# One double load removed, two loads moved: rows of q, k and v in an attention and feed-forward kernel

## The chip, the cores and the metric

The kernel runs on one core of a Trainium2 chip. A core has a matrix engine (TensorE, PE), a vector engine (VectorE, DVE), a scalar engine (ScalarE, ACT), a general engine (GpSimd, POOL) and an engine that mostly issues transfers (SyncE, SP). Each runs its own list of instructions in order; they meet through semaphores. Sixteen DMA engines move data between the chip's memory (HBM) and the on-chip memory (SBUF); transfers are issued from the lists of SyncE, ScalarE and GpSimd. The metric is the device time of one execution in microseconds, as the median of several runs.

## The reference

Attention with a squared ReLU in place of softmax, over 8 batches of 12 heads, 448 positions and 64 elements a head; then a feed-forward layer with a leaky ReLU whose slope is different for each hidden unit.

```python
# q, k, v: (8, 12, 448, 64)
scores = scale * np.matmul(q, k.transpose(0, 1, 3, 2))
attn = np.maximum(scores, 0.0) ** 2 / S
attn_out = np.matmul(attn, v)
x = attn_out.transpose(0, 2, 1, 3).reshape(B * S, H * D)      # (3584, 768)
h = x @ w_in                                                 # (3584, 2048)
g = np.maximum(h, 0.0) + alpha * np.minimum(h, 0.0)
out = g @ w_out                                              # (3584, 768)
```

## The kernel before

The heads are worked on four at a time. Such a group is called a quad: with NG = 3 quads to a batch and 8 batches there are NQ = 24, numbered 0 to 23. Each quad passes through these steps.

Its rows are loaded by GpSimd, with a cast from float32 to bfloat16. q and k have three buffers each, v has seven:

```python
raw_pool = ctx.enter_context(tc.tile_pool(name="raw", bufs=3))
v_pool = ctx.enter_context(tc.tile_pool(name="v", bufs=7))
perm_pool = ctx.enter_context(tc.tile_pool(name="perm", bufs=2))
T_pool = ctx.enter_context(tc.tile_pool(name="T", bufs=4))
...
def load_qk(n):
    b, g = divmod(n, NG)
    for name, src in (("q", q), ("k", k)):
        t = raw_pool.tile([128, 2, NJ, D], BF16, tag=name, name=f"{name}raw")
        flat = src[b].rearrange("(m two) (pp j) d -> (two pp) m (j d)", two=2, j=NJ)
        nc.gpsimd.dma_start(out=t.rearrange("p m j d -> p m (j d)"), in_=flat[:, 2 * g:2 * g + 2])   # L91
        raw[(n, name)] = t

def load_v(n):                  # the same for v, into vraw[n]                                        # L98
    ...
```

Scores need q and k with the 64 elements of a head on the partitions, so both are transposed. Quads 0 to 5 are transposed by TensorE (`turn_pe`, L144, with copies out of PSUM at L147). Quads 6 to 23 are reordered by VectorE into a tile `perm` and transposed by a DMA that SyncE issues:

```python
def turn_dma(n):
    p = perm_pool.tile([128, 2, NJ, 2, D], BF16, tag="perm", name="perm")
    for i, name in enumerate("qk"):
        nc.vector.tensor_copy(p[:, i], raw.pop((n, name)).rearrange("p s j d -> p j s d"))            # L155
    t = T_pool.tile([128, 2, NJ, 128], BF16, tag="T", name="T")
    nc.sync.dma_start_transpose(out=t.rearrange("p a j c -> p (a j) c"),
                                in_=p.rearrange("p a j s d -> p (a j s d)"))                          # L157
    T[n] = t
```

Then come seven chunks of scores (`score_mm`, L169), a ReLU (L178 on ScalarE, L180 on VectorE), a square (L185), the product with v (`attnv`, L195), and once all three quads of a batch are there, the first layer (`f1`, matmuls at L229, outputs at L237 and L238) and the second (`f2`, matmuls at L252, a copy at L254, a store at L260).

The schedule is written out by hand, and TensorE's order is the order of the calls. The part that matters here is the end of the first phase, where batch 0's second layer and batch 1's attention meet, and the first-layer block of batch 1 behind it:

```python
def prepare(n):
    if n < NQ:
        turn_dma(n)
    if n + 2 < NQ:
        load_qk(n + 2)
        load_v(n + 2)
...
sc(ch(4, 5, 7))
turn_pe(5)
sq()
load_qk(8)                      # L347: quad 8
load_v(8)
f2(0, 1, 0)
...                             # scores of quad 5, attnv(4), more of f2
early = []
for ff in range(4):
    ps = take_bank()[:, :S]
    f1_mm(ps, 1, ff, range(4))
    early.append(ps)
    if ff == 1:
        attnv(5)
for ff in range(KF):            # KF = 16
    if ff < 4:
        f1_mm(early[ff], 1, ff, range(4, KM))
        f1_out(early[ff], 1, ff)
    else:
        f1(1, ff)
    if ff in (1, 5, 9):
        prepare(6 + ff // 4)    # turns quad 6, 7, 8; loads quad 8 (again), 9, 10
f2(0, 3, 0)
run(some(3))                    # scores of quad 6 and on, three chunks at a time
f2(0, 3, 1)
f2(0, 0, 1)
run(some(3))
f2(0, 1, 1)
run(some(3))
f2(0, 2, 1)
f2(0, 4, 0)
prepare(9)                      # L398: turns quad 9, loads quad 11
burst(6)                        # three chunks, attnv(6), three chunks
...
prepare(10)                     # turns quad 10, loads quad 12
burst(8)
...                             # batches 2 to 7 in the same manner
```

Quad 8 is loaded at L347, and once more by `prepare(6)`. The second tile replaces the first under `raw[(8, "q")]`, `raw[(8, "k")]` and `vraw[8]`, so the first is not read by anything.

Of the kernel before, what the change touches and what calls it, by code (L numbers as in the profile page):

```python
# [20 lines left out]
def kernel(  # L21
# [17 lines left out]
    NQ = B * NG  # L39
# [46 lines left out]
# [8 lines that stand above are left out]
    def load_v(n):  # L94
        b, g = divmod(n, NG)
        t = v_pool.tile([128, 2, NJ, D], BF16, tag="v", name="vraw")
        flat = v[b].rearrange("(m two) (pp j) d -> (two pp) m (j d)", two=2, j=NJ)
        nc.gpsimd.dma_start(out=t.rearrange("p m j d -> p m (j d)"), in_=flat[:, 2 * g:2 * g + 2])  # L98
        vraw[n] = t
# [52 lines left out]
# [8 lines that stand above are left out]
# [67 lines left out]
    def f1_mm(ps, b, ff, ks):  # L227
        for km in ks:
            nc.tensor.matmul(ps, w_in_sb[:, km // 2, km % 2, bass.ts(ff, 128)],  # L229
                             xT[b][:, km // 2, km % 2, :],  # L230
                             start=(km == 0), stop=(km == KM - 1))

    def f1_out(ps, b, ff):
        if b % 2 == 0 and ff == 0:
            gT[b // 2] = g_pool.tile([128, KF, 2 * S], BF16, tag="g", name="gT")
        neg = neg_pool.tile([128, S], F32, tag="neg", name="neg")
        nc.scalar.activation(neg, ps, ACTF.Relu, scale=-1.0)  # L237
        nc.vector.scalar_tensor_tensor(gT[b // 2][:, ff, (b % 2) * S:(b % 2) * S + S],  # L238
                                       neg, beta_sb[:, ff:ff + 1], ps, ALU.mult, ALU.add)
        sq(1)  # L240

    def f1(b, ff):
        ps = take_bank()[:, :S]
        f1_mm(ps, b, ff, range(KM))
        f1_out(ps, b, ff)

    def f2(sb, c, hf, parts=((0, HALF),)):
        o = o_pool.tile([128, HALF], F32, tag="o", name="osb")
        for lo, hi in parts:
            ps = take_bank()[:, :hi - lo]  # L250
            for ff in range(KF):
                nc.tensor.matmul(ps, gT[sb][:, ff, bass.ts(c, 128)], w_out_sb[:, hf, ff, lo:hi],  # L252
                                 start=(ff == 0), stop=(ff == KF - 1))
            nc.scalar.copy(o[:, lo:hi], ps)  # L254
            for u in range(2):
                blk = 2 * c + u
                b, j = 2 * sb + blk // NJ, blk % NJ
                rows = out[b * S:(b + 1) * S].rearrange("(pp j) d -> j pp d", j=NJ)
                eng = nc.scalar if u and hi - lo < HALF else nc.sync
                eng.dma_start(out=rows[j][:, hf * HALF + lo:hf * HALF + hi], in_=o[64 * u:64 * u + 64, lo:hi])  # L260
# [53 lines left out]
    def f1s(b, lo, hi):  # L314
        for ff in range(lo, hi):
            f1(b, ff)

    def prepare(n):
        if n < NQ:
            turn_dma(n)  # L320
        if n + 2 < NQ:
            load_qk(n + 2)
            load_v(n + 2)

    f1s(0, 2, 3)
    turn_pe(3)
# [54 lines left out]
    for ff in range(KF):  # L381
# [3 lines that stand above are left out]
        else:  # L385
            f1(1, ff)
        if ff in (1, 5, 9):
            prepare(6 + ff // 4)
    f2(0, 3, 0)
    run(some(3))  # L390
    f2(0, 3, 1)
# [4 lines left out]
    f2(0, 2, 1)  # L396
    f2(0, 4, 0)
    prepare(9)  # L398
    burst(6)
    f2(0, 4, 1)  # L400
    f2(0, 5, 0)
    burst(7)
    f2(0, 5, 1)
    f2(0, 6, 0)
    prepare(10)
    burst(8)
    f2(0, 6, 1)
# [56 lines left out]
```

## Time and profile before

| what | value |
|---|---|
| time, median of 3 runs | 392.98 us (392.55 to 398.75) |
| span of the profiled execution | 389.5 us |
| TensorE busy | 378.2 us, 97% |
| VectorE busy | 263.9 us, 68% |
| ScalarE busy | 207.5 us, 53% |
| GpSimd busy | 65.5 us, 17% |
| moved by DMA | 43.75 MB, 112 GB/s on average |
| GpSimd's DMA queue | 23.04 MB, 40.4% of the 16 engines' span |
| first DMA queue of SyncE and ScalarE | 19.65 MB, 25.7% |
| loads of q, k, v by GpSimd | 24, 24 and 25, of 224 KB each as written |
| median from issue to landing of those loads | 4.8, 6.7 and 7.4 us |
| transposing transfers | 18, 7.6 us median to landing (3.4 to 14.6) |

The profile is of one execution, and its times count from the first instruction. A line such as L91 is a line of the kernel. In the tables of waits and in timelines, an arrow points to what an engine waited for: the last event that released it. Busy time of TensorE (PE) is that of its matmuls; they are pipelined, so their mean duration (353 ns at L229) is longer than their spacing. A transfer has an issue, which takes time on the issuing engine, and a landing.

### The profile page before, as it was taken

To read this page: it belongs to the slowest core of one execution; us is meant where nothing else is said; L and a number is where in the kernel's file an instruction comes from. 1 tells how busy PE (TensorE), PEld (TensorE's weight loads), DVE (VectorE), ACT (ScalarE), POOL (GpSimd) and SP (SyncE) were. 2 spreads that over 40 slices of the span, in tenths; PEclk is the share of its full clock that TensorE was granted. 3 is DMA by queue.
4 is the path that set the end of the run, shared out by engine and by line. 5 is a ranking of instruction groups with operands and counts; after the bars stand their busy time and mean duration, and the time that the engine had idled before them with its cause. 6 is when DMAs were issued, how large, how long until landed. Compare 5 with 4: busy or idle time off the path is not lost.

```text
span 389.5 us, 7956 instructions
## 1 busy us (share of the span) xinstructions
PE 378.2 (97%) x3228; PEld 216.0 (55%) x3228; DVE 263.9 (68%) x418; ACT 207.5 (53%) x332; POOL 65.5 (17%) x97
## 2 busy tenths in 40 slices
PE   7779999999999999999999999999999999999996
PEld 5435454555665556645655456654666546655564
DVE  3977966865777777868756687878756786735300
ACT  4966566545546546555455554655644565524311
POOL 7557212520202040202202022102000000000000
PEclk9999999999999999999999999999999999999999
DMA  9999999996859089574939259490832311120023
GB/s 181 191 202 204 206 211 206 167 195 139 134 86 144 29 129 169 82 98 73 159 89 146 55 53 176 95 153 8 164 82 51 80 24 46 42 61 2 12 72 82
DMA packets 71909, 43.75 MB, mean 112 GB/s; under 512 B 38208, under 2 KB 71872, under 8 KB 71872
## 3 DMA queue, kind: packets, MB, share of 16 engines
q0 software_dynamic: 27312, 23.04, 40.4%
q1 hardware_dynamic: 44128, 19.65, 25.7%
q8 instruction: 25, 0.41, 0.4%
q10 hardware_dynamic: 432, 0.56, 0.4%
q14 instruction: 12, 0.10, 0.1%
HBM read 47.00 MB, written 11.01 MB: 149 GB/s over the span
## 4 chain that ended last, share of the span: by engine, by line
PE 88%; ACT 5%; DVE 3%; issue 2%; DMA 1%; ACTq 0%
PE psum L252 38%; PE psum L229 36%; PE psum L169 7%; PE psum L195 6%; ACT rl L178 4%; DVE at L185 2%; DMA qfirst<-in_q_dram 1%; DVE T L147 1%; PE psum L144 1%; ACT xT L205 1%; DVE rl L180 1%; DVE gT L238 0%; ACT osb L254 0%; DVE qraw L127 0%; ACTq L260 0%
## 5 line engine op out<-in xcount | busy, mean ns | idle before, releaser
L252 PE MATMUL psum<-w_out_sb,gT 128*128 128x384 bf16 (+2 forms) x912 | 150.7, 323 | 0.2
L229 PE MATMUL psum<-xT,w_in_sb 128*128 128x448 bf16 x768 | 148.7, 353 | 1.1 <-ACT xT L205 0.6
L252 PEld LDWEIGHTS <-gT 128*128 128x128 bf16 x912 | 87.6, 98 | 61.5 <-issue 6.7
L229 PEld LDWEIGHTS <-w_in_sb 128*128 128x128 bf16 x768 | 74.2, 98 | 71.8 <-issue 4.4
L238 DVE SCALAR_TENSOR_TENSOR gT<-neg,beta_sb,psum 128x448 bf16<-128x448 f32 x128 | 84.5, 678 | 41.3 <-ACT neg L237 40.9
L237 ACT ACTIVATE neg<-psum 128x448 f32<-128x448 f32 x128 | 69.3, 546 | 70.3 <-PE psum L229 64.7
L178 ACT ACTIVATE rl<-psum 128x896 bf16<-128x896 f32 x120 | 102.9, 928 | 1.2 <-PE psum L169 1.2
L185 DVE TENSOR_TENSOR at<-rl 128x896 bf16<-128x896 bf16 x168 | 94.1, 618 | 3.5 <-ACT rl L178 3.4
L254 ACT COPY osb<-psum 128x384 f32<-128x384 f32 (+2 forms) x57 | 27.0, 474 | 97.5 <-PE psum L252 94.0
L180 DVE TENSOR_SCALAR rl<-psum 128x896 bf16<-128x896 f32 x48 | 52.1, 1086 | 37.1 <-PE psum L169 37.1
L91 POOL DMA_DIRECT2D qraw<-in_q_dram x24 | 17.2, 718 | 190.2 <-DVE perm L155 170.1
L169 PE MATMUL psum<-T 64*64 64x448 bf16 x672 | 44.7, 355 | 3.8 <-DVE T L147 1.4
L195 PE MATMUL psum<-at,vraw 64*64 64x448 bf16 x672 | 37.9, 351 | 0.7 <-ACT rl L178 0.2
L169 PEld LDWEIGHTS <-T 64*64 64x64 bf16 x672 | 20.9, 105 | 21.6 <-issue 14.6
L195 PEld LDWEIGHTS <-vraw 64*64 64x64 bf16 x672 | 24.8, 106 | 10.9 <-issue 3.7
L206 DVE TENSOR_SCALAR xT<-psum 128x448 bf16<-128x448 f32 x22 | 13.7, 625 | 14.3 <-PE psum L195 7.2
L91 POOL DMA_DIRECT2D kraw<-in_k_dram x24 | 17.3, 721 | 6.9 <-PE psum L169 3.3
L98 POOL DMA_DIRECT2D vraw<-in_v_dram x25 | 18.0, 722 | 1.2 <-DMA w_in_sb<-in_moe_w_in_dram 0.4
L205 ACT ACTIVATE xT<-psum 128x448 bf16<-128x448 f32 x22 | 12.0, 545 | 5.4 <-PE psum L195 5.4
L155 DVE COPY perm<-qraw 128x896 bf16<-128x896 bf16 x18 | 11.0, 612 | 0.4 <-DMA T<-perm 0.4
L108 POOL DMA_DIRECT2D w_in_sb<-in_moe_w_in_dram x16 | 10.0, 628 | 7.4 <-DMA vraw<-in_v_dram 2.5
L155 DVE COPY perm<-kraw 128x896 bf16<-128x896 bf16 x18 | 11.0, 609 | 0.0
(19 smaller groups left out, 35.5 us busy)
## 6 DMA issues: line engine op xcount, KB each, us to landing
out_dram<-osb SPq DMA_DIRECT2D x110, 96.0 KB, 2.3
vraw<-in_v_dram POOLq DMA_DIRECT2D x25, 224.0 KB, 7.4
qraw<-in_q_dram POOLq DMA_DIRECT2D x24, 224.0 KB, 4.8
kraw<-in_k_dram POOLq DMA_DIRECT2D x24, 224.0 KB, 6.7
w_in_sb<-in_moe_w_in_dram POOLq DMA_DIRECT2D x16, 192.0 KB, 8.7
w_out_sb<-in_moe_w_out_dram POOLq DMA_DIRECT2D x2, 1536.0 KB, 18.6
qfirst<-in_q_dram SPq DMA_DIRECT2D x1, 448.0 KB, 4.4
kfirst<-in_k_dram ACTq DMA_DIRECT2D x1, 448.0 KB, 4.7
```

Of the source, the lines that this page charges most:

```text
L91: nc.gpsimd.dma_start(out=t.rearrange("p m j d -> p m (j d)"), in_=flat[:, 2 * g:2 * g + 2])
L155: nc.vector.tensor_copy(p[:, i], raw.pop((n, name)).rearrange("p s j d -> p j s d"))
L169: nc.tensor.matmul(ps[64 * c:64 * c + 64, r, :S], t[64 * r:64 * r + 64, 1, j, 64 * c:64 * c + 64], t[64 * r:64 * r + 64, 0, :, 64 * c:64 * ...
L178: nc.scalar.activation(rl, ps[:, :, :S], ACTF.Relu)
L180: nc.vector.tensor_scalar(rl, ps[:, :, :S], 0.0, None, ALU.max)
L185: nc.vector.tensor_tensor(a, rl, rl, ALU.mult)
L195: nc.tensor.matmul(ps[64 * s:64 * s + 64, r, :S], vv[64 * r:64 * r + 64, s, j, :], a[64 * r:64 * r + 64, s], start=(j == 0), stop=(j == NJ ...
L229: nc.tensor.matmul(ps, w_in_sb[:, km // 2, km % 2, bass.ts(ff, 128)], xT[b][:, km // 2, km % 2, :], start=(km == 0), stop=(km == KM - 1))
L237: nc.scalar.activation(neg, ps, ACTF.Relu, scale=-1.0)
L238: nc.vector.scalar_tensor_tensor(gT[b // 2][:, ff, (b % 2) * S:(b % 2) * S + S], neg, beta_sb[:, ff:ff + 1], ps, ALU.mult, ALU.add)
L252: nc.tensor.matmul(ps, gT[sb][:, ff, bass.ts(c, 128)], w_out_sb[:, hf, ff, lo:hi], start=(ff == 0), stop=(ff == KF - 1))
L254: nc.scalar.copy(o[:, lo:hi], ps)
```

## The change

The rows of quad 8 are loaded once instead of twice, and in the first-layer block of batch 1 the calls that load quads 9 and 10 stand after the three calls that transpose quads 6, 7 and 8, at ff = 13, where before each transposing call was followed by a load. The aim is to spare a transfer that nothing reads, and to let the three transposing transfers go without loads beside them. `prepare` keeps its meaning for quads 9 and later.

```diff
+    def load(n):
+        if n < NQ:
+            load_qk(n)
+            load_v(n)
+
     def prepare(n):
         if n < NQ:
             turn_dma(n)
-        if n + 2 < NQ:
-            load_qk(n + 2)
-            load_v(n + 2)
+        load(n + 2)
...
         else:
             f1(1, ff)
         if ff in (1, 5, 9):
-            prepare(6 + ff // 4)
+            turn_dma(6 + ff // 4)
+        if ff == 13:
+            load(9)
+            load(10)
     f2(0, 3, 0)
```

## The prediction

> **What bounds the kernel now.** I read the page from the top first: the busy shares, the strips of forty slices (9.7 us each), the chain that ended last.
>
> ```profile
> PE 378.2 (97%) x3228; PEld 216.0 (55%) x3228; DVE 263.9 (68%) x418; ACT 207.5 (53%) x332; POOL 65.5 (17%) x97
> ...
> PE   7779999999999999999999999999999999999996
> ...
> DMA  9999999996859089574939259490832311120023
> ...
> PE 88%; ACT 5%; DVE 3%; issue 2%; DMA 1%; ACTq 0%
> PE psum L252 38%; PE psum L229 36%; PE psum L169 7%; PE psum L195 6%; ACT rl L178 4%; DVE at L185 2%; DMA qfirst<-in_q_dram 1%; DVE T L147 1%; PE psum L144 1%; ACT xT L205 1%; DVE rl L180 1%; DVE gT L238 0%; ACT osb L254 0%; DVE qraw L127 0%; ACTq L260 0%
> ```
>
> TensorE is busy for 378.2 of 389.5 us, and 88% of the chain is TensorE; the only DMA in it is the first load of q. The DMA engines are also near full for the first nine slices, to about 88 us, so "the transfers are full" and "TensorE is full" are both on the page, and the stage that is changed has to decide between them. That stage is the first-layer block of batch 1 (L381 to L394) and what follows until quads 9 and 10 are used. The chain of waits in order of time shows it:
>
> ```profile
> 66.38 16.75 PE psum L229 x88
> 83.14 2.60 PE psum L252 x16
> 85.74 0.69 PE psum L169 x12
> 86.43 5.31 PE psum L252 x32
> ```
>
> 88 matmuls of the first layer without a break, then f2(0, 3, 0), then the first three score chunks of quad 6, then more f2. No step between them is a wait. The busy time by stretches says the same of the whole affected region (columns: stretch, its length, busy time and instructions of PE, PEld, DVE, ACT, POOL, granted clock, DMA share, GB/s):
>
> ```profile
> 66.00:83.20 17.20, 17.20 (x94) 8.90 (x94) 13.08 (x22) 8.45 (x17) 8.59 (x12) 1.00 1.12 177
> 83.20:122.60 39.40, 39.40 (x369) 23.58 (x368) 27.15 (x43) 21.28 (x32) 4.28 (x6) 1.00 0.76 131
> ```
>
> PE is busy for 17.20 of 17.20 and 39.40 of 39.40 us, at full clock. A wait that could be removed isn't there.
>
> Then I asked who issues and who waits. GpSimd's timeline gives each load's issue:
>
> ```profile
> 54.63 0.72 POOL L91 DMA_DIRECT2D qraw<-in_q_dram  x1 [5.05 <-PE psum L144]
> ...
> 66.72 0.72 POOL L91 DMA_DIRECT2D qraw<-in_q_dram  x1 [6.63 <-DMA qraw<-in_q_dram]
> 68.24 0.72 POOL L91 DMA_DIRECT2D kraw<-in_k_dram  x1 [0.80 <-DMA kraw<-in_k_dram]
> 68.95 0.72 POOL L98 DMA_DIRECT2D vraw<-in_v_dram  x1
> 71.10 0.72 POOL L91 DMA_DIRECT2D qraw<-in_q_dram  x1 [1.43 <-DVE perm L155]
> ...
> 74.52 0.72 POOL L91 DMA_DIRECT2D qraw<-in_q_dram  x1 [1.28 <-DVE perm L155]
> ...
> 78.95 0.72 POOL L91 DMA_DIRECT2D qraw<-in_q_dram  x1 [1.36 <-DVE perm L155]
> ```
>
> I matched these to the program's order: 54.63 is quad 8 (L347), 66.72 is quad 8 again, out of prepare(6). The first copy's tile is dropped unread, so the second takes the same buffer and has to wait 6.63 us for the first to land. 71.10 is quad 9, 74.52 quad 10, and 78.95 already quad 11, though prepare(9) stands far below in the text (L398). So GpSimd isn't paced by the place of a call among the matmuls. It runs through its own list and stops only where a buffer isn't free: with three buffers per name, quad 9 waits for the copy of quad 6 to perm (VectorE, 70.19 us), 10 for that of quad 7 (73.60), 11 for that of quad 8 (78.03).
>
> The last view is VectorE's timeline, with the only wait for a transposing transfer in the whole run:
>
> ```profile
> 70.19 0.61 DVE L155 COPY perm<-qraw 128x896 bf16<-128x896 bf16 x1
> ...
> 78.03 0.62 DVE L155 COPY perm<-qraw 128x896 bf16<-128x896 bf16 x1 [0.41 <-DMA T<-perm]
> ```
>
> **What the Trainium skill says.** "DMA: Bandwidth & Descriptors", section "Anatomy of one DMA — SWDGE (gpsimd) path", says that the DMA engines don't wait on semaphores: a wait happens on the issuing sequencer, before dispatch. The trace agrees: the GpSimd loads start right after the perm copy that frees their buffer (71.10 after a copy that runs from 70.19 to 70.80). The same page, "Queues, rings and completion order", says that each DMA engine goes round-robin over the queues that have work, packet by packet, so a load and a transposing transfer in flight together share the engines. The trace agrees as far as it goes: the three transposing transfers of quads 6 to 8, issued at 71.4, 74.8 and 80.3 us, took 6.5, 14.6 and 10.7 us to land, while the shortest of all 18 took 3.4 us. "SBUF — State Buffer", section "SBUF: two separate sides", lists TensorE's SBUF ports as its own, with contention only between VectorE and GpSimd or among DMA; a matmul should then not slow down under DMA traffic. Here the 88 matmuls under full DMA took 16.75 us, 190.3 ns each; 96 matmuls of the last batch (18.16 us, with the DMA digits at 1) took 189.2 ns each. That is 0.6%, or 0.1 us over the 88.
>
> **The change, part by part.** I compared the order of instructions, and the counts that each waits for, in the two built programs.
>
> *Removed:* one issue each of q, k and v, 3 x 0.72 us = 2.15 us of GpSimd, from 66.72 on, and the 6.63 us that it waited ahead of them. GpSimd then waits for the perm copy of quad 6 instead. The DMA work: the page's queue of GpSimd carries 23.04 MB in 40.4% of 389.5 us, 157.4 us, so 6.83 us per MB on all 16 engines; three times 224 KB is 0.69 MB, or 4.7 us of all engines, all between 66.7 and about 88 us. On the path: nothing, since TensorE has no gap there.
>
> *Moved:* the loads of quads 9 and 10, in the text. In the built programs, the q and k loads of quad 9 wait for VectorE's instructions 87 and 88 before and after; those of quad 10 for 93 and 94 in both; those of quad 11 for 99 and 100 in both. The order on PE, VectorE, ScalarE and SyncE is the same instruction for instruction; what differs in their waits is only which of eight numbered DMA semaphores a load signals. So quad 9 is still issued at about 71 and quad 10 at about 74.5 us, ahead of the landing of the transposing transfers at 77.9, 89.4 and 91.0 us (issue plus landing time), and not behind them. This half of the change is void: the place in the text doesn't hold a queue back, only a wait does.
>
> *Follows from it:* less traffic beside the three transposing transfers. They may land up to 4.7 us earlier in all. T of quad 6 landed at 77.9 and is first used at 85.7 us; quad 7 landed at 89.4 and is used at 95.1; quad 8 landed at 91.0 and is used at 103. Slacks of 7.8, 5.7 and 12 us: earlier is of no use. VectorE's wait of 0.41 us for perm's buffer may go; VectorE was idle for 4.1 of the 17.2 us in this stretch and TensorE didn't wait for it. SyncE's issues may be shorter (three transposes, 17.3 us of its queue), so the stores behind them start before 88.8 us; ScalarE doesn't wait for a store there.
>
> Sum: 0 on the path from the removed load, 0 from the move, 0 to 0.1 us from matmuls with less traffic beside them. 392.98 - 0.1 is 392.9; I say 392.8, with the rest for a small effect on the tail of VectorE that I can't work out.
>
> **The rivals.** *First: the doubled load keeps the chain back through the DMA engines.* For it: DMA digits of 9 up to 88 us, and a landing of 14.6 us. If quad 7's T were late, removing 4.7 us of traffic would give up to 4.7 us, 1.2%: about 388.3. Against it: PE busy 39.40 of 39.40 us and a slack of 5.7 us on the tightest of the three. It needs waits that this trace doesn't have.
>
> *Second: the later loads come too late.* If the loads did move behind quad 8's transposing transfer, they would be issued from about 81 us on, and quads 9 and 10 are copied to perm at about 98 and 116 us. With the median landing times of 4.8 to 7.4 us there would be some 10 us left even then. And if quad 11 were pushed back, it is needed later still. It makes the time longer only if a queue of loads builds up; I give that at most 1 us.
>
> *Third: a new collision.* Quad 8's q, k and v now come from the single load issued at 54.6 to 59.4 us. Its q had landed by 66.7 and its k by 68.2 us (the doubled loads waited for just that), some 10 us ahead of their use at 78.0. And v, with seven buffers, gets one more buffer of slack. Nothing for a slower time.
>
> **Range and chances.** Since no instruction of the four other engines changes its place, what decides is the spread between executions. Of the three runs before, two lie 0.43 us apart and the third 1.5% above; the profiled execution took 391.3 us. So plus and minus 1.2 us: 391.6 to 394.0. Faster by over 2% needs 7.9 us, more than twice TensorE's idle time after the first 66 us (11.3 us in all, 7.5 of it before 66 us): 0.01. Slower by over 2% needs a wait of 8 us that nothing here points to: 0.005. Within 2%: 0.985.
>
> **What would show it right or wrong.** Right: TensorE still busy for about 378.2 us and without a gap from 66 to 122 us; GpSimd busy for some 63.3 us, with 23 q loads, 23 k loads and 24 v loads; the issue at 66.72 gone, and the next still at about 71, 74.5 and 78.5 us, not at 81 or later; q, k and v queue at 22.35 MB; the three transposing transfers landing sooner than 6.5, 14.6 and 10.7 us, with TensorE indifferent to it. Wrong: loads of quad 9 issued after 80 us, a gap on TensorE before a score matmul (L169) put down to T, or a first-layer block that takes more or less than 16.75 us by over 0.3 us. The prediction would fail as a whole if traffic slows matmuls or their weight loads in a way that the busy time of PE hides.

## The result and the profile after

The changed kernel takes 391.43 us (median of 4 executions, 391.24 to 391.54). The kernel before, beside it, takes 393.24 us (4 executions, 392.55 to 398.75). The ratio is 0.9959, with a 95% interval of 0.994 to 0.9979: faster by 0.4%. Ratios here are taken over the executions within 1.5% of a kernel's fastest one; where I count executions, I count all.

The profile after hardly differs from the one before. First its page, the lines that answer to those shown of before:

```profile
span 389.7 us, 7952 instructions
...
PE 378.6 (97%) x3228; PEld 216.5 (56%) x3228; DVE 263.8 (68%) x418; ACT 207.5 (53%) x332; POOL 63.3 (16%) x94
...
DMA  9999999696859089574949269490932311120023
...
q0 software_dynamic: 26496, 22.35, 39.3%
```

The span is 389.7 us against 389.5. GpSimd lost 2.2 us of work, its queue 0.69 MB, and the eighth digit of the DMA strip (68 to 78 us) fell from 9 to 6. Next the GpSimd timeline of the changed kernel:

```profile
54.78 0.72 POOL L91 DMA_DIRECT2D qraw<-in_q_dram  x1 [5.02 <-PE psum L144]
...
71.25 0.72 POOL L91 DMA_DIRECT2D qraw<-in_q_dram  x1 [10.97 <-DVE perm L155]
...
74.67 0.72 POOL L91 DMA_DIRECT2D qraw<-in_q_dram  x1 [1.28 <-DVE perm L155]
...
79.22 0.72 POOL L91 DMA_DIRECT2D qraw<-in_q_dram  x1 [2.41 <-DVE perm L155]
```

The issue at 66.7 us is gone; quads 9, 10 and 11 are issued where they were. Last, the chain of waits of the changed kernel in the same stage:

```profile
66.53 16.75 PE psum L229 x88
83.29 2.60 PE psum L252 x16
85.89 0.69 PE psum L169 x12
86.58 5.31 PE psum L252 x32
```

Each piece is as long as before, to 0.01 us; all start 0.15 us later. VectorE's wait for perm's buffer is there too, 0.52 us instead of 0.41:

```profile
78.29 0.62 DVE L155 COPY perm<-qraw 128x896 bf16<-128x896 bf16 x1 [0.52 <-DMA T<-perm]
```

So the two profiled executions are equal, and the medians of plain executions are 1.8 us apart. A difference that one trace of each kernel can't show must lie in how executions of the same kernel differ. That is what the experiments are about.

### The profile page after: what moved, and what is told of

It is laid out like the page before. It is cut to its first block, busy times and chain, and to the rows that moved or that the text cites. A ratio compares the mean times of both kernels' runs of the same rounds, so it can differ in the third digit from the quotient of the medians.

```text
span 389.7 us, 7952 instructions
## 1 busy us (share of the span) xinstructions
PE 378.6 (97%) x3228; PEld 216.5 (56%) x3228; DVE 263.8 (68%) x418; ACT 207.5 (53%) x332; POOL 63.3 (16%) x94
## 3 DMA queue, kind: packets, MB, share of 16 engines
q0 software_dynamic: 26496, 22.35, 39.3%
## 4 chain that ended last, share of the span: by engine, by line
PE 87%; ACT 5%; DVE 3%; DMA 2%; issue 2%; ACTq 0%
PE psum L252 37%; PE psum L229 36%; PE psum L169 7%; PE psum L195 6%; ACT rl L178 4%; DVE at L185 2%; DMA qfirst<-in_q_dram 1%; DVE T L147 1%; PE psum L144 1%; ACT xT L205 1%; DVE rl L180 1%; DMA out_dram<-osb 1%; DVE gT L238 0%; ACT osb L254 0%; DVE qraw L127 0%
## 5 line engine op out<-in xcount | busy, mean ns | idle before, releaser
L229 PE MATMUL psum<-xT,w_in_sb 128*128 128x448 bf16 x768 | 148.6, 353 | 1.1 <-ACT xT L205 0.6
L229 PEld LDWEIGHTS <-w_in_sb 128*128 128x128 bf16 x768 | 74.2, 98 | 71.8 <-issue 4.4
L238 DVE SCALAR_TENSOR_TENSOR gT<-neg,beta_sb,psum 128x448 bf16<-128x448 f32 x128 | 84.3, 677 | 41.3 <-ACT neg L237 40.9
L169 PEld LDWEIGHTS <-T 64*64 64x64 bf16 x672 | 20.9, 105 | 21.6 <-issue 14.6
L91 POOL DMA_DIRECT2D kraw<-in_k_dram x23 | 16.6, 720 | 5.7 <-PE psum L169 3.4
```

Source lines behind the costliest of these rows:

```text
L169: nc.tensor.matmul(ps[64 * c:64 * c + 64, r, :S], t[64 * r:64 * r + 64, 1, j, 64 * c:64 * c + 64], t[64 * r:64 * r + 64, 0, :, 64 * c:64 * ...
```

## The experiments

Two theories at the start. *Traffic*: the useless load costs time in some executions of the kernel before that the profile of one good execution doesn't show. *Draw*: the kernel before is no slower, and three or four of its executions were unlucky.

**e1_same_again.** The kernel before, with no edit but a comment.

> The kernel before once more, as a kernel of its own: what two copies of one program differ by. If the measured 0.41% (1.8 us) belongs to the removed load, this copy gives a ratio of 1.000 within 0.15%, about 393.2 us. If the 0.41% lies in which executions of the kernel before were drawn, this copy comes out below the kernel before too, by 0.2% or more (392.5 us or less).

Measured: median 393.45 us over 22 executions, 391.21 to 401.27; ratio 1.001, 0.9976 to 1.0043. The kernel before on the same chip: 391.14 to 402.27 over 75, median 392.0. The figures fit the first expectation and not the second, but the interval is 0.7% wide, so this run can't tell a gain of 0.4% from none. What it shows is the width itself. The two copies share a floor of 391.2 us, 9 of 22 and 20 of 75 of their executions lie above 395 us, and over 75 executions the median of the kernel before is 392.0 us, not the 393.24 of the first four.

**e2_changed_again.** The changed kernel, with no edit but a comment.

> The changed kernel once more. If the gain is the change's own: ratio 0.996, 391.4 us again. If it is the draw: a ratio that moves to 0.998 or more.

Measured: median 391.36 us, 391.15 to 392.65 over 22; ratio 0.9976, 0.9953 to 0.9998. The time is that of the first expectation, the ratio is nearer to the second: part of the first 1.8 us was the draw of four executions of the kernel before. The floor is the same, and none of 22 is above 392.7 us. The gain that is left isn't a faster execution. It is the absence of long ones.

**e3_single_load.** Only the second load of quad 8 left out:

```diff
-        if n + 2 < NQ:
+        if n + 2 < NQ and n != 6:
             load_qk(n + 2)
             load_v(n + 2)
```

> The kernel before with the second load of quad 8 left out and nothing moved. Since the moved calls wait for the same events as before, this should equal the changed kernel: 391.4 us if the removed load is what counts, and issues at 71, 74.5 and 78.5 us. If the moving of quads 9 and 10 is what counts, this stays at 393.2 us.

Measured: 391.37 us, 391.15 to 392.56 over 22; ratio 0.9971, 0.9948 to 0.9994. It equals the changed kernel, and its loads of quads 9, 10 and 11 are issued at 71.11, 74.53 and 79.59 us.

**e4_moved_only.** The changed kernel with the double load put back:

```diff
             turn_dma(6 + ff // 4)
+        if ff == 1:
+            load(8)
         if ff == 13:
```

> The double load of quad 8 kept, the loads of quads 9 and 10 moved as in the change. If the move is void: 393.2 us, ratio 1.000 within 0.15%, with issues at 66.7, 71, 74.5 and 79 us as before. If the move carries the gain: 391.4 us.

Measured: median 392.38 us, 391.2 to 403.28 over 22, 9 of them above 395; ratio 0.9983, 0.9951 to 1.0016. Issues at 66.47, 71.02, 74.44 and 80.41 us. It behaves as the kernel before does. So the gain is the removed load's, and moving the two calls shows no effect.

**What a long execution looks like.** The profiled execution of e1 was one of the long ones, with a span of 398.5 us. Its chain of waits:

```profile
66.45 5.02 PE psum L229 x26
71.47 16.61 DMA T<-perm
...
88.21 1.15 DVE perm L155 x2
89.36 3.56 DVE gT L238 x6
...
93.46 1.26 PE psum L169 x12
94.72 5.92 PE psum L252 x32
```

A transposing transfer has come into the chain: that of quad 6, issued at 71.47 us, which took 16.6 us to land. In the profile of the kernel before it took 6.5. Who waited for whom in the same execution, from 66 to 98 us (columns: engine and line, what it waited for, us in all, times, longest):

```profile
DVE perm L155 <- DMA T<-perm: 10.5, 1, 10.5
ACT neg L237 <- DVE gT L238: 10.4, 2, 9.7
PEld L252 <- DVE gT L238: 8.0, 6, 5.6
...
PE psum L252 <- DVE gT L238: 5.2, 1, 5.2
```

Read from the top: perm has two buffers, so the copy of quad 8 needs the one that quad 6's transfer is reading, and VectorE waits 10.5 us for the landing. VectorE works in order, so the outputs of the first layer (L238) behind that copy wait too. ScalarE stops for them. TensorE runs through its 88 first-layer matmuls, since the results of the six outputs that are still to be written fit into the kernel's eight PSUM banks, and starts f2(0, 3, 0), whose block of 128 tokens reaches into batch 1 and needs all 16 of those outputs. There it stops, as its timeline shows:

```profile
83.04 1.79 PE L252 MATMUL psum<-w_out_sb,gT 128*128 128x384 bf16 x10
90.00 3.46 PE L252 MATMUL psum<-w_out_sb,gT 128*128 128x384 bf16 x6 [5.17 <-DVE gT L238]
93.39 0.96 PE L169 MATMUL psum<-T 64*64 64x448 bf16 x8
```

The score chunk starts at 93.39 us, against 85.67 in the profile before; less the 0.07 us by which this execution was later already, 7.65 us are lost. Some 1.2 us more go after the stop: the score chunk took 1.26 us instead of 0.69, the 32 matmuls of f2 behind it 5.92 instead of 5.31. TensorE's granted clock was 0.50 from 90 to 95 us, and 1.00 again from 96 us on. That makes 8.8 of the 9.0 us between the two spans.

The clock also dips without such a stop. In the profiled execution of e5 (below) it was 0.50 from 23 to 26 us, long before the load in question; eight matmuls of L229 took 3.07 us there instead of 1.67, and all that follows is 1.2 us later. So part of the spread, up to some 392.6 us, has another cause than the load. The changed kernel seems to have it too: two executions of e2 (392.64 and 392.65 us) have the same mean clock, 0.996, as that execution of e5 (392.49 us).

How much of VectorE's wait is free can be read across traces. It was 1.9 us in e4 and 2.5 us in e9 (below), at spans of 389.4 and 389.6, and TensorE didn't stop. In e6 it was 3.4 us, at a span of 390.0, and TensorE stopped briefly:

```profile
PE psum L252 <- DVE gT L238: 0.2, 1, 0.2
```

Its score chunk started at 86.16 us; less the 0.10 us by which e6 was later already, that is a loss of 0.39 us, so 3.0 us of the wait were free. In e1 it was 2.9 us (10.5 less 7.65). So some 3 us are free, and what is above is lost nearly one for one.

**e5_perm_three.** If that is the mechanism, a third buffer for perm must cure it with the double load kept:

```diff
-    perm_pool = ctx.enter_context(tc.tile_pool(name="perm", bufs=2))
+    perm_pool = ctx.enter_context(tc.tile_pool(name="perm", bufs=3))
```

> The kernel before, double load kept, with three buffers for perm instead of two: VectorE's copy of quad 8 no longer waits for the transposing transfer of quad 6. Theory (a late landing of quad 6's transposing transfer stops VectorE, and TensorE behind it): the executions of 396 to 402 us go; what a landing at 88 us can still cost is TensorE's own wait for that tile, 88 - 85.7 = 2.4 us, so no execution above 395 us and a median near 391.4. Rival (more traffic costs time whatever waits on it, or the chip is disturbed by itself): the spread stays as in the kernel before, about a third of executions above 394 us.

Measured: 391.27 us, 391.11 to 393.93 over 22, none above 395, where the kernel before on the same chip has 26 of 62 (median 392.74). Ratio 0.9979, 0.9957 to 1.0001. So the long executions go, as the theory had it. The dearest one is 2.8 us above the floor, 0.4 us more than the 2.4 us that TensorE's own wait for the tile was worked out to; three lie at 393.2 to 393.9 us, and what they waited for isn't shown, as none of them was profiled. The loads and transfers ahead of quad 8's copy are issued in the same order as before, so the third buffer should leave the late landings as they are and only take the wait for them away; the one trace of e5, with a landing of 7.8 us, doesn't show a late one.

**e6_triple_load.** One more useless load of quad 8:

```diff
             load_qk(n + 2)
             load_v(n + 2)
+        if n == 6:
+            load_qk(n + 2)
+            load_v(n + 2)
```

> Quad 8 loaded three times: one more useless load of q, k and v (4.7 us of all DMA engines by the page's rate) in the same place. Theory: quad 6's transposing transfer lands late in most executions, not in a third; the median is 396 us or more. Rival (the spread has nothing to do with this load): the same spread as before, median near 392 to 393.5.

Measured: median 391.4 us, 391.13 to 401.24 over 22, only 2 above 395 (26 of 62 of the kernel before on the same chip); ratio 0.9979, 0.9955 to 1.0002. More useless bytes, fewer long executions: the expectation failed, and with it the idea that the amount of traffic decides. What the third load also did is push quad 9's loads from 71 to 73.7 us, as they queue behind it.

**e7_held_single and e8_held_double.** Quads 9 and 10 really held until quad 8's transposing transfer has landed, in the changed kernel and in e4:

```diff
+    seen = singles.tile([128, 1], BF16)
...
         if ff == 13:
+            nc.gpsimd.tensor_copy(seen, T[8][:, 0, 0, :1])
             load(9)
             load(10)
```

> The changed kernel, with GpSimd reading one column of quad 8's transposed tile ahead of the loads of quads 9 and 10, so that they are really held until the transposing transfers of quads 6 to 8 have landed. If transposing transfers suffer from loads beside them: the three land within some 6 us of their issue each, quad 9 is issued at about 85 us instead of 71, in time for its use at 98.6 us, and the time stays at 391.3 us with no execution above 392.7. If quad 9 comes too late this way: 393 us or more.

> The double load of quad 8 kept, the loads of quads 9 and 10 really held as in e7. If it takes the loads of quads 9 and 10 beside the transposing transfer of quad 6 to make it late: no execution above 392.7 us, median 391.4, though the useless load is there. If the useless load alone makes it late: the spread of the kernel before, a third of the executions above 394 us.

Measured: e7 393.47 us, 392.69 to 394.31 over 14; e8 393.33 us, 392.8 to 394.92 over 16; ratios 1.0031, 1.0017 to 1.0045, and 1.0031, 1.0007 to 1.0055. In e7 the three transposing transfers took 4.1, 4.0 and 4.0 us to land (6.6, 15.1 and 11.3 in the changed kernel), so what the change's text intends does make them fast. In e8, with the useless load in place, they took 6.7, 4.9 and 4.0 us, and none of 16 executions was above 395 us, where at 26 of 62 some seven were to be expected: with quad 9's loads held, the useless load alone made no long execution.

But neither time is the expected one. Both medians lie 2 us above the changed kernel's, and the loss isn't where the edit is. The stage from 66 to 122 us is as before. Of the 2.1 us between the spans of e7 and e2, 1.3 are lost at 190 us, on a later transposing transfer. First e2, then e7 (whose lines lie one further down), around its issue:

```profile
179.56 1.48 SPq L157 DMA_TRANSPOSE T<-perm  x1
179.97 0.72 POOL L91 DMA_DIRECT2D kraw<-in_k_dram  x1
```

```profile
180.44 1.79 SPq L158 DMA_TRANSPOSE T<-perm  x1
180.44 0.72 POOL L92 DMA_DIRECT2D kraw<-in_k_dram  x1
...
191.10 0.38 PE L170 MATMUL psum<-T 64*64 64x448 bf16 x4 [1.16 <-DMA T<-perm]
```

In e2 the transfer was issued 0.41 us ahead of the k load and landed in 6.9 us. In e7 it was issued beside it and landed in 10.6 us, and TensorE waited. VectorE's copy had ended 0.07 us before the issue in the one and 0.49 us before it in the other; why SyncE was later I couldn't find. e8 has the same picture (both at 180.20, 10.5 us). It is no matter of one draw: this transfer took 6.8 to 7.3 us in all eleven kernels without the added instruction, and 10.5 to 10.7 us in the three that have it (e7, e8 and e11 below).

**e9_double_qk.** The double load without its v:

```diff
             load_qk(n + 2)
-            load_v(n + 2)
+            if n != 6:
+                load_v(n + 2)
```

> The kernel before with quad 8's q and k loaded twice, but its v once: the last of the three useless transfers, issued at 69 us and landed at 74, which is in flight when quad 6's transposing transfer starts at 71.4. Theory (useless bytes still in flight at that moment, with quad 9's loads right behind them, make the landing late): few or no executions above 395 us, median 391.4. Rival (any part of the double load is enough): a third of the executions above 395, as in the kernel before.

Measured: 391.39 us, 391.21 to 397.08 over 14, 1 above 395; ratio 0.9995, 0.9972 to 1.0019. The kernel before on this chip: 8 of 52 above 395, median 391.57. At that share two were to be expected in 14, so this one is inconclusive.

**e10_twice_nine.** As many useless bytes, but quad 9's:

```diff
         if ff == 13:
             load(9)
+            load(9)
             load(10)
```

> Quad 8 loaded once, quad 9 twice: as many useless bytes as in the kernel before, but issued from about 76 us on, after quad 6's transposing transfer has started. If the amount of traffic in the stage makes the executions of 396 us and more: they are there again, in a third. If only what is in flight ahead of that transfer does: none above 395 us, median 391.4.

Measured: 391.3 us, 391.11 to 392.56 over 22, none above 395; ratio 0.998, 0.9966 to 0.9993. The same bytes in the same stage, issued from 76.2 us on, made no long execution, where some three of 22 were to be expected (the kernel before on this chip: 8 of 52). That points to what is in flight as quad 6's transfer starts. It doesn't settle it, since this edit also puts off quad 10's loads, from 74.5 to 80.3 us.

**e11_held_six.** As e8, with `T[6]` in place of `T[8]`, so that only quad 6's transfer is sheltered.

> Double load kept, quads 9 and 10 held by a GpSimd read of quad 6's transposed tile alone, until about 76 us. If quad 9's loads beside that transfer are needed to make it late: no execution above 395 us. The floor may lie 1.5 us over that of the kernel before, as in the two held kernels, if that came from the added instruction; if it came from the late loads (83 us), it is gone and the median is 391.4.

Measured: 394.57 us, 393.47 to 395.23, but over 7 executions only, 1 above 395 (by 0.23); ratio 1.0053, 1.003 to 1.0076. Quad 6's transfer took 4.4 us with quad 9's loads held until 77.7 us, though the useless load was ahead of it. Seven executions can't say whether the long ones are gone: at 8 of 52, one was to be expected. The floor is no lower than in e7 and e8, with transposing transfers in its chain at 181 and 231 us, though quad 9's loads came 6 us earlier than there. So the added instruction, or what it shifts, is the likelier reason for the floor than the late loads.

**e12_single_perm3.** The changed kernel with e5's edit on top.

> The changed kernel with three buffers for perm: both cures at once. TensorE bounds both, so 391.3 us, no faster than either alone (ratio to the kernel before 0.996 to 0.998), and no execution above 392.7.

Measured: 391.37 us, 391.13 to 393.21 over 22; ratio 0.9994, 0.9984 to 1.0005. No faster than the changed kernel, as expected. The ratio isn't the expected one, since the median of the kernel before is 391.57 us on this chip; and two executions are above 392.7 us (392.73 and 393.21). Their mean clock was 0.996, as in the profiled execution of e5, so the dip of the clock told of above can explain 1.2 us of them. The floor is the same in all kernels without an added instruction: 391.1 to 391.2 us.

| kernel | executions | above 395 us | lowest |
|---|---|---|---|
| before, beside e1 to e4 | 75 | 20 | 391.14 |
| before, beside e5 to e8 | 62 | 26 | 391.20 |
| before, beside e9 to e12 | 52 | 8 | 391.16 |
| before again (e1) | 22 | 9 | 391.21 |
| moved only (e4) | 22 | 9 | 391.20 |
| three loads of quad 8 (e6) | 22 | 2 | 391.13 |
| double load without its v (e9) | 14 | 1 | 391.21 |
| changed (first result and e2) | 26 | 0 | 391.15 |
| single load only (e3) | 22 | 0 | 391.15 |
| double load, three perm buffers (e5) | 22 | 0 | 391.11 |
| quad 9 twice (e10) | 22 | 0 | 391.11 |
| single load, three perm buffers (e12) | 22 | 0 | 391.13 |
| held, single load (e7) | 14 | 0 | 392.69 |
| held, double load (e8) | 16 | 0 | 392.80 |
| held for quad 6 alone, double load (e11) | 7 | 1 | 393.47 |

The three groups of the kernel before are from three chips; a kernel's share of long executions is to be compared with that of its own group.

## Why the prediction was right and wrong

**Right: within 2%, and why a good execution can't be shorter.** TensorE's time without a gap sets the floor. Removing the load left it at 391.15 us, against 391.14. The counts came as forecast too: TensorE busy for 378.6 us and without a gap in this stage, GpSimd for 63.3 us, 22.35 MB in its queue.

**Right: the move is void.** The issue times of after, e3 and e4 show it (quad 9 at 71.25, 71.11 and 71.02 us, against 71.10 before), and e4's spread. GpSimd waits for the perm copies, wherever the call stands.

**Wrong: the size, 392.8 against 391.43 us.** The measured time lies 0.17 us under the stated range. The sum had 0 on the path for the removed load; it was worth 1.8 us of the median in the first result, 0.6 us of the median on the chip of e2 (392.0 against 391.36), and 2 us of the mean there (393.42 against 391.45). Part of the miss is luck of the draw: the 392.98 us that the sum started from was the middle one of three executions out of a spread of 391.1 to 402.3, and the median of the kernel before came out at 392.0, 392.74 and 391.57 us on the three chips. I took that spread for noise around one time; what lay above 395 us came with the very load that the change removes.

**The step that failed** is the one under "Follows from it": "VectorE's wait of 0.41 us for perm's buffer may go; VectorE was idle for 4.1 of the 17.2 us in this stretch and TensorE didn't wait for it." The line was the right one, shown as the only wait for a transposing transfer, and I read its 0.41 us as a fixed quantity. It was one draw: the same wait was 1.9, 2.5, 3.4 and 10.5 us in the traces of e4, e9, e6 and e1, all with the double load, a part of it or more of it; without it, it was 0.5 to 1.0 us (after, e2, e3, e10). The slack was the thing to work out: how late may quad 6's transfer land before VectorE's outputs hold TensorE? The runs say some 3 us of waiting. With 0.41 used, some 2.5 us were left, less than the spread of landing times that the page gave (3.4 to 14.6).

**The first rival was right in kind and wrong in place.** It had the doubled load act through a late T, and I turned it down by the slack between T's landing and TensorE's use of it: 7.8 us for quad 6, and 5.7 for the tightest. But TensorE isn't the first to suffer from a late quad 6. VectorE is: it wants perm's buffer back at 77.6 us (the copy at 78.0, less its wait of 0.4), 8 us before TensorE wants T, and has only some 3 us to give.

**Wrong too: shorter landings.** The transfers of quads 6 to 8 took 6.6, 15.1 and 11.3 us in the profile after, not less than 6.5, 14.6 and 10.7. In the profile before, the useless load was issued at 66.7, 68.2 and 69.0 us and landed within 3.7 to 5.0 us, so its k and v were still in flight, until 72.4 and 74.0 us, when quad 6's transfer began at 71.4; in that execution they cost it nothing.

**What stays open.** Why quad 6's transfer takes 6 to 10 us in most traces and 16.6 in one isn't shown. In the one trace that has it, quad 8's first q took 12.5 us to land instead of 11.8, so the useless q was issued at 67.50 instead of 66.72 and its v was in flight until 75.9; quad 9's k and v, issued at 71.9 and 72.6, took 15 us as well. From 78 to 83.2 us all DMA together moved 100 GB/s there, against 196 in the profile before, at a busy share that was no lower (1.46 against 1.24): the engines weren't idle, they got less done. e3 shows that the useless load is needed for long executions. e8 says that quad 9's loads (or those of 10 and 11, which it holds too) are needed as well, and e10 points to bytes that come later being harmless. How the DMA engines turn that into 16.6 us isn't seen in these traces.

## What to carry to other kernels

Look for waits that are nearly zero, on an in-order engine that feeds the bound one, and ended by a transfer: work out how much later the transfer may land before the bound engine stops, and compare that with the spread of its landing times, not with the one that the trace shows. A useless transfer can be free in the best execution and still be the difference between a spread of 1.5 us and one of 11. Here a call's place in the source didn't delay an issue; only a wait in its queue did.

## What I had not expected of the hardware

Tenths of a microsecond in a transposing transfer's issue went with microseconds in its landing. The transfer at 180 us, issued 0.4 us ahead of a load of k, took 6.8 to 7.3 us in eleven traces; issued together with that load it took 10.5 to 10.7 us in three; and in e7, with all loads held back, the transfers of quads 6 to 8 took 4.0 to 4.1 us. That the moment of issue is the cause isn't shown, since the three traces also share the added instruction. And after a stop of 5.2 us TensorE's granted clock was 0.50 for some 6 us, which added 1.2 us to the 7.6 us that were lost until then. The mean over the stage, 0.91 from 83.2 to 122.6 us, hides it.
